# Two work tiles for GpSimd, a one-pass range check and a new order of the steps in an RWKV kernel

## The chip, the cores and the metric

The kernel runs on one core of a Trainium2 chip. The metric is the device time of one execution in microseconds (us), taken as the median of several runs. The core has five engines, each of which works through its own list of instructions strictly in order: TensorE (PE in the profile, with its weight loads as PEld), VectorE (DVE), ScalarE (ACT), GpSimd (POOL) and SyncE (SP), which here only issues DMA transfers. An instruction whose input isn't ready holds up everything that stands behind it on its engine.

## The reference

A linear attention with a state (RWKV) over 768 time steps, and behind it a feed-forward layer that the program calls MoE. Cut to what is computed:

```python
for t in range(S):                       # 4 batches x 8 heads, state 40 x 40 each
    y[:, :, t] = einsum('bhd,bhde->bhe', r_t, state)
    Sa = einsum('bhde,bhe->bhd', state, a_t)
    state = state * w_t[:, :, None, :] - einsum('bhd,bhe->bhde', Sa, b_t)
    state = state + einsum('bhd,bhe->bhde', v_t, k_t)
x = y.transpose(0, 2, 1, 3).reshape(4, 768, 320)
x_prev = x shifted by one step in time
xk = mu_k * x + (1 - mu_k) * x_prev ;  xr = mu_r * x + (1 - mu_r) * x_prev
out = sigmoid(xr @ w_r) * (relu(xk @ w_k) ** 2 @ w_v)     # 320 -> 1024 -> 320
```

All is float32.

## The kernel before

**Chunks.** Time is cut into 12 chunks of 64 steps (`NK`, `C`). A chunk is worked on in two halves `p` of the batches, 16 batch-and-head pairs each. Inside a chunk the recurrence becomes matrix products and one triangular solve; only a chain of small products carries the state from one chunk to the next.

**What is prepared for a chunk k, per half.** `load_wab` brings w, a, b and k of the chunk in one transfer (`wab`, 836 KB, two buffers in all). `check` has ACT look whether w lies inside the range in which the chunk form is safe; it writes into the tile `pe` that the next instruction overwrites, and sums into `beyond`. `front` is four pieces on DVE: a running product of w (L295), its inverse and a scan backwards (L298, L299), the scaling of a (L305) and of b and k (L307). `psc` (scores, L322) has PE multiply them, and ACT and DVE copy the parts to `sn` and `az`. `pkt` (L337) transposes `kb`, which lies in the `wab` buffer and is its last reader. So the next `wab` load of that half waits for `pkt`.

**The triangular solve.** `tri_out` (L351) writes blocks of `sn` to DRAM (`tx`, 64 KB each, runs of 128 bytes), `tri` (L366) loads them back in another layout into `TA`, and GpSimd solves in `TD` with 60 small instructions (L367 to L380), `tri_store` (L356) writes `TD` out (`ty`), and `tri_back` (L360) brings it into `sn`. There is one `TA` and one `TD` for all chunks.

**The chain of a chunk** (`chain`, `put`): the links z (L402), T (L408), L (L414), U (L420) and s (L426), each for both halves, with a copy on ACT between one and the next. T and U read what `tri_back` wrote. `put` (L441) hands the values on, and GpSimd multiplies the carried state by the decay into `mc` (L449), which `pmt` transposes in the next chunk. `pgh` (L472) and `py` (L488, L493) form the chunk's output, and `send_x` (L510, L512) sends it into the tile `x`, five transfers in runs of 256 bytes.

**MoE.** `Mix` works on one chunk's `x`: three differences (`diff`, L140), six mixed tiles, and 18 units of PE work (eight `ph`, eight `pv` pairs, two `pr`, as the generator `products` cuts them). `advance` emits one unit and, where they lie ahead, one of the mixes. Its weights come as 18 pieces that `convert` turns from 64-bit numbers into two 32-bit halves (`some_weights`).

**The order** is written out by hand. `STEP` holds 25 slots, numbered from 0, that are run for every chunk k. A word is a call; its last digit is the half. `z T L U s` are the links, `put pmt pgh py` belong to chunk k. `psc` and `pkt` are for chunk k+2, `w` is `load_wab` and `Q` is `check` for k+3, `r` (`load_rv`, 416 KB) and `v` load for k+1. `to` is `tri_out` and `tl` the load and solve of `tri` for k+2, `ts` is `tri_store` and `tk` `tri_back` for k+1, `x` is `send_x`. `F` emits one piece of a front, `M` one unit of MoE (before chunk `LAG`, now and then a weight piece). Copies and masks are put off to the end of the slot (`later`).

**DMA.** All loads and stores of a step are issued by SP in the order of the slots. There are eight completion semaphores, used in turn, so a transfer is issued only when the one eight places ahead of it has landed.

## Time and profile before

| | us |
|---|---|
| median of 3 runs (809.21 to 810.81) | 810.1 |
| the profiled execution | 807.6 |
| its span, from the first to the last instruction | 805.9 |
| busy: PE / DVE / POOL / ACT | 553.7 / 445.7 / 416.0 / 330.4 |
| mean granted TensorE clock | 0.867 of full speed |

The profile gives for each engine its busy time, and for each wait what ended it. No engine is busy for more than 69% of the span, so the time is set by engines that wait for each other. A step of the main loop is the time from one chunk's link z to the next chunk's. The first link z starts 84.0 us into the span and the last at 727.3 us; the last matmuls end close to the end of the span. So there is a head of some 84 us, eleven steps, and a last step with its tail of 79 us.

### The profile page before, as it was taken

How to read it: one execution, taken by the hardware profiler on the slowest of the kernel's cores; microseconds unless marked ns; L12 is line 12 of the kernel's file. 1: busy time of each engine (PE TensorE's matmuls, PEld its weight loads, DVE VectorE, ACT ScalarE, POOL GpSimd, SP SyncE). 2: the span in 40 equal slices, each digit the busy share in tenths (PEclk: the TensorE clock that was granted, in tenths of full speed). 3: DMA queues.
4: the chain of work that ended last, by engine and by line, in shares of the span. 5: the costliest groups of instructions: out<-in, count | busy, mean ns of one | idle time of the engine just before them, and what ended most of it. 6: DMA issues, size and time to landing. Idle time of an engine off the chain costs nothing.

```text
span 805.9 us, 24880 instructions
## 1 busy us (share of the span) xinstructions
PE 553.7 (69%) x10658; PEld 502.4 (62%) x10658; DVE 445.7 (55%) x772; ACT 330.4 (41%) x841; POOL 416.0 (52%) x815
## 2 busy tenths in 40 slices
PE   0302276236459979598598598596698799898966
PEld 0201266235458869487587487585687688797865
DVE  3754687469457467285385275392384492443441
ACT  1222241243144564363453444552453553545433
POOL 4086286088185187295494483484583582840000
PEclk9999999996758989699699679799589779797979
DMA  5245823842822732823814714714715625232010
GB/s 122 51 112 109 185 64 57 200 107 63 155 60 51 146 70 53 176 60 47 188 28 77 158 31 88 145 39 75 149 40 95 130 49 91 63 72 62 2 39 21
DMA packets 120321, 71.16 MB, mean 88 GB/s; under 512 B 96547, under 2 KB 110843, under 8 KB 117707
## 3 DMA queue, kind: packets, MB, share of 16 engines
q1 hardware_dynamic: 117710, 63.00, 38.5%
q10 hardware_dynamic: 2493, 6.49, 3.1%
q8 instruction: 85, 1.39, 0.8%
q14 instruction: 33, 0.27, 0.1%
HBM read 52.98 MB, written 10.22 MB: 78 GB/s over the span
## 4 chain that ended last, share of the span: by engine, by line
PE 42%; DMA 21%; DVE 12%; POOL 8%; SPq 6%; ACT 6%; issue 5%; ACTq 0%; DVEq 0%
DMA wab<-in_wab_dram 12%; PE ph L113 12%; PE pv L113 8%; POOL ttmp L373 4%; POOL td L376 4%; DMA x<-xp 3%; PE py L488 3%; PE py L493 2%; PE pgh L472 2%; PE psc L322 2%; PE ch L408 2%; PE ch L414 2%; PE ch L426 2%; PE pr L113 1%; DMA ty<-td 1%
## 5 line engine op out<-in xcount | busy, mean ns | idle before, releaser
L373 POOL TENSOR_TENSOR ttmp<-ta,td 128x30 f32<-128x30 f32 (+4 forms) x360 | 189.7, 527 | 28.3
L376 POOL TENSOR_TENSOR td<-td,ttmp 128x30 f32<-128x30 f32 (+4 forms) x360 | 176.7, 491 | 28.2
L113 PE MATMUL ph<-xk,wkh 120*128 120x256 f32 x480 | 110.8, 332 | 96.0 <-ACT hf L91 66.5
L113 PEld LDWEIGHTS ph<-xk,wkh 120*128 120x128 f32 x480 | 82.8, 220 | 104.9 <-ACT hf L91 70.1
L367 POOL TENSOR_SCALAR_AFFINE_SELECT td<-ta 64x512 f32<-64x512 f32 x24 | 19.5, 813 | 243.3 <-DMA ta<-tx 227.4
L91 DVE TENSOR_TENSOR hl<-hf,hh 128x256 fp32r<-128x256 f32 x96 | 43.1, 449 | 150.9 <-ACT hh L91 144.2
L322 PE MATMUL psc<-az,wab 40*64 40x64 f32 x1536 | 39.0, 253 | 63.4 <-DVE wab L307 53.9
L91 ACT ACTIVATE hf<-ph 128x256 f32<-128x256 f32 x96 | 36.9, 384 | 98.3 <-PE ph L113 98.3
L322 PEld LDWEIGHTS psc<-az,wab 40*64 40x64 f32 x1536 | 33.7, 163 | 69.0 <-issue 55.0
L91 ACT ACTIVATE pe<-wab,limit 104x512 f32<-104x512 f32 x48 | 34.6, 721 | 100.6 <-DMA wab<-in_wab_dram 96.0
L113 PE MATMUL ph<-xk,wkl 120*128 120x256 f32 x288 | 73.6, 312 | 1.4 <-DMA xk<-xk 1.4
L113 PE MATMUL pv<-wvh,hh 128*128 128x320 f32 x192 | 70.8, 369 | 0.0
L113 PE MATMUL pv<-wvh,hl 128*128 128x320 f32 x192 | 63.9, 333 | 0.0
L113 PE MATMUL pv<-wvl,hh 128*128 128x320 f32 x192 | 63.7, 332 | 0.0
L113 PEld LDWEIGHTS ph<-xk,wkl 120*128 120x128 f32 x288 | 56.0, 222 | 1.9 <-DMA xk<-xk 1.9
L408 PE MATMUL ch<-zs,sn 32*32 32x40 f32 x768 | 23.4, 236 | 45.6 <-ACT zs L91 35.0
L408 PEld LDWEIGHTS ch<-zs,sn 32*32 32x32 f32 x768 | 21.5, 141 | 48.1 <-ACT zs L91 45.8
L295 DVE TENSOR_TENSOR_SCAN pe<-wab,first 104x520 f32<-104x520 f32 x24 | 32.8, 1366 | 22.9 <-ACT pe L91 22.9
L91 ACT COPY vu<-ch 32x320 f32<-32x320 f32 x96 | 40.0, 417 | 9.1 <-PE ch L408 6.8
L113 PEld LDWEIGHTS pv<-wvh,hh 128*128 128x128 f32 x192 | 40.0, 209 | 4.2
L402 PE MATMUL ch<-vu,az 128*64 128x40 f32 (+1 forms) x768 | 31.9, 257 | 14.8 <-DMA vu<-in_vt_dram 14.8
L91 ACT ACTIVATE hf<-hf 128x256 f32<-128x256 f32 x96 | 40.1, 417 | 3.0
(95 smaller groups left out, 1207.2 us busy)
## 6 DMA issues: line engine op xcount, KB each, us to landing
wab<-in_wab_dram SPq DMA_DIRECT2D x24, 835.7 KB
vr<-in_rvd_dram SPq DMA_DIRECT2D x24, 416.0 KB
ta<-tx SPq DMA_DIRECT2D x24, 256.0 KB
vu<-in_vt_dram SPq DMA_DIRECT2D x24, 256.0 KB
out_dram<-sig SPq DMA_DIRECT2D x48, 80.0 KB
tx<-sn SPq DMA_DIRECT2D x48, 64.0 KB
ty<-td SPq DMA_DIRECT2D x24, 128.0 KB
sn<-ty SPq DMA_DIRECT2D x48, 64.0 KB
```

The lines of the kernel that those rows point to most:

```text
L91: f(*args, **kw)
L113: nc.tensor.matmul(out, lhsT=left[i][g], rhs=right[j][g], start=start and k == 0, stop=stop and k == len(terms) - 1)
L295: nc.vector.tensor_tensor_scan(out=pe.rearrange("p x t -> p (x t)"), data0=w[:, 0:SP], data1=first, initial=0.0, op0=ALU.mult, op1=ALU.add)
L322: nc.tensor.matmul(to[64 * y:64 * y + 64, x], lhsT=kb[r0:r1, x, y], rhs=az[r0:r1, i, x], start=True, stop=True)
L367: nc.gpsimd.affine_select(out=TD[h], in_=TA[h, i::2], compare_op=ALU.is_gt, fill=0.0, base=-i, pattern=[[-2, 16], [1, 32]], channel_multip ...
L373: nc.gpsimd.tensor_tensor(out=tmp, in0=TA[:, s:s + 1, s + 1:].broadcast_to([128, rows, n]), in1=TD[:, 0:rows, s:s + 1].broadcast_to([128, ...
L376: nc.gpsimd.tensor_tensor(out=TD[:, 0:rows, s + 1:], in0=TD[:, 0:rows, s + 1:], in1=tmp, op=ALU.subtract)
L402: mm(c3[64 * i:64 * i + 64, x], lhsT=az[0:kr[i], i, x], rhs=vu[0:kr[i], i, x, 0:HD], start=(x == 0), stop=True, skip_group_check=(x > 0))
L408: mm(c3[a:a + 32, x], lhsT=sn[a:a + 32, x, 0:32], rhs=zs[a:a + 32, x], start=True, stop=True)
L414: mm(c3[a + 32:a + 64, x], lhsT=sn[a:a + 32, x, 32:64], rhs=vu[a:a + 32, i, x, 0:HD], start=False, stop=True, skip_group_check=True)
L426: mm(c3[r0:r1, x], lhsT=kt[:, i, x], rhs=vu[:, i, x, 0:HD], start=(x == 0), stop=True, skip_group_check=(x > 0))
L488: nc.tensor.matmul(y[r0:r0 + n, 2 * x + q], lhsT=mk[:, x, i, q, 0:n], rhs=r[:, x, i], start=(x == 0 and q == 0), stop=False, skip_group_ch ...
```

## The change

- `TA` and `TD` exist twice, and chunk k uses the pair k modulo 2.
- `check` is one pass: Square of w - 0.9, summed; the sums are compared with 0.8 at the end, and the padding in the input is 0.9. It was two passes of Relu against 0.6 and 1.6.
- `fronts` becomes one list in the order of the checks; `F` always takes the next piece of the oldest.
- `STEP` is rewritten: `psc` is at slots 7 and 9, right behind U, where it was at 10 and 13; `to` at 10 and `tl` at 14, ahead of both `w`, where they were at 16 and 20; `ts` and `tk` are behind `w0` and `r0`; the check of half 0 is at slot 23 and that of half 1 (`q`) at slot 1 of the next step, where their passes were at 19 and 20, and 23 and 24; F stands in slots 0 to 6 and 24. There are 19 M in it, where there were 20.
- MoE starts at slot 12 of chunk 1, where it started with chunk 2.
- The head is rewritten: the first loads are split, the fronts of one half are laid over the scores of the other, and the loads for chunks 0 to 2 come earlier.
- `kt` has four buffers, where it had six.

```diff
-LAG = 2
+MOE_FROM = (1, 12)

 STEP = [x.split() for x in (
-    "z0 z1 F", "M", "T0 T1 F", "M pmt0", "L0 L1 F", "M pmt1 F", "U0 U1", "M F", "s0 s1 put0 F", "M put1", "M psc0 v F",
-    "M pgh0 F", "M", "M psc1", "M py0 ts", "M pgh1", "M pkt0 to", "M py1", "M pkt1 tk w0", "M r0 Q0", "M tl w1 Q0", "M x r1",
-    "M", "M Q1", "M Q1")]
+    "z0 z1 F", "M F q1", "T0 T1 F", "M pmt0 F", "L0 L1 F", "M pmt1 F", "U0 U1 F", "M psc0", "s0 s1", "M psc1", "M put0 to",
+    "M put1 v", "M pgh0", "M", "py0 tl", "M pgh1", "M pkt0", "M py1 w0 r0", "M pkt1 ts", "M w1 r1", "M", "M tk", "M x",
+    "M Q0", "M F")]
...
-            TA = att.tile([128, 32, 32], F32, name="ta")
-            TD = att.tile([128, 16, 32], F32, name="td")
+            TAS = [att.tile([128, 32, 32], F32, name=f"ta{i}") for i in range(2)]
+            TDS = [att.tile([128, 16, 32], F32, name=f"td{i}") for i in range(2)]
...
-                later(0, nc.scalar.activation, out=d["pe"][:, :, 1:], in_=w, func=AF.Relu, scale=(-1.0, 1.0)[i],
-                      bias=limit[:, i:i + 1], accum_out=beyond[:, i, k, p:p + 1])
+                later(0, nc.scalar.activation, out=d["pe"][:, :, 1:], in_=w, func=AF.Square, bias=limit,
+                      accum_out=beyond[:, k, p:p + 1])
+                fronts.append((k, p, front(k, p)))
+
+            def front_some(n):
+                while n > 0 and fronts:
+                    if next(fronts[0][2], 1) is None:
+                        n -= 1
+                    else:
+                        fronts.pop(0)
...
-                    nc.sync.dma_start(ty[:, i::2], TD[64 * i:64 * i + 64])
+                    nc.sync.dma_start(ty[:, i::2], TDS[k % 2][64 * i:64 * i + 64])
...
-                tx = st.pop((k, "tx"))
+                tx, TA, TD = st.pop((k, "tx")), TAS[k % 2], TDS[k % 2]
...
-            AHEAD = dict(r=(1, load_rv), w=(3, load_wab), Q=(3, check_next), psc=(2, scores), pkt=(2, pkt))
+            AHEAD = dict(r=(1, load_rv), w=(3, load_wab), Q=(3, check), q=(2, check), psc=(2, scores), pkt=(2, pkt))
...
+            def to_scores(k):
+                for p in range(2):
+                    check(k, p)
+                    flush()
+                front_some(4)
+                psc(k, 0)
+                front_some(2)
+                flush()
+                pkt(k, 0)
+                front_some(2)
+                psc(k, 1)
                 flush()
...
-                    load_wab(0, p)
+                    load_wab(0, p, ((0, WP), (WP, WP + 3 * G * C)))
                 for j in range(2):
-                    load_w(j)
...
+                    load_w(j, nc.sync)
+                to_scores(0)
+                tri_out(0)
+                load_wab(1, 0)
+                pkt(0, 1)
                 flush()
                 some_weights(1)
                 tri(0)
...
+                load_wab(1, 1)
+                some_weights(2)
+                to_scores(1)
+                tri_out(1)
+                pkt(1, 1)
                 flush()
...
+                load_wab(2, 0)
                 load_v(0)
                 for p in range(2):
                     load_rv(0, p)
...
+                tri(1)
+                load_wab(2, 1)
...
+                some_weights(1)
                 tri_store(0)
-                tri(1)
                 tri_back(0)
...
                             if what == "M":
-                                if k >= LAG:
+                                if (k, n) >= MOE_FROM:
                                     advance()
-                                elif n % 2 == 0:
+                                elif n % 2 == 0 or k > 0:
                                     some_weights(1)
```

**Where it moves the transfers.** SP before, around the late slots of the step of chunk 4; `wab` is the load for chunk 7, `tx` and `ta` belong to the solve of chunk 6, `ty` and `sn<-ty` to that of chunk 5:

```order
L356 DMA ty<-td 1024x1x32 x2
L91 DMA xk<-xk 40x256
L351 DMA tx<-sn_4010 32x16x32 x4
L360 DMA sn_3158<-ty 32x16x32 x4
L277 DMA wab_0_4380<-in_wab_dram 104x2057
L91 DMA out_dram<-sig 64x320 x4
L389 DMA vr_0_4406<-in_rvd_dram 104x4x256
L366 DMA ta<-tx 64x1024 x2
L277 DMA wab_1_4493<-in_wab_dram 104x2057
L510 DMA x_4515<-xp_4211 40x12x64 x2
L512 DMA x_4515<-xp_4211 40x4x64 x3
L389 DMA vr_1_4522<-in_rvd_dram 104x4x256
```

The same place of SP in the changed program:

```order
L362 DMA tx<-sn_4029 32x16x32 x4
L394 DMA vu<-in_vt_dram 64x2x512
L395 DMA vu<-in_vt_dram 64x2x512
L90 DMA xr<-xr 40x256
L377 DMA ta_114<-tx 64x1024 x2
L277 DMA wab_0_4524<-in_wab_dram 104x2057
L400 DMA vr_0_4526<-in_rvd_dram 104x4x256
L367 DMA ty<-td_117 1024x1x32 x2
L277 DMA wab_1_4575<-in_wab_dram 104x2057
L400 DMA vr_1_4577<-in_rvd_dram 104x4x256
L371 DMA sn_3195<-ty 32x16x32 x4
L521 DMA x_4618<-xp_4336 40x12x64 x2
```

The store and load ahead of GpSimd's solve (`tx`, `ta`) now stand ahead of both `wab` loads and no longer behind the store `ty` of the solve before; `ty` has moved behind the first `wab` and `vr`, and its way back into `sn` behind the second ones.

**Where it moves VectorE's work.** DVE before, at the beginning of the step of chunk 5; `pe_0`, `wab_0` and `az_102` are front pieces of chunk 7, half 0, `diff` the first MoE work on chunk 4's `x`:

```order
L295 SCALAR_TENSOR_TENSOR pe_0_4408<-wab_0_4380,first 104x520
L140 TENSOR_TENSOR diff<-x_4515 120x256 x3
L298 RECIPROCAL inv<-pe_0_4408 104x8
L299 SCALAR_TENSOR_TENSOR wab_0_4380<-wab_0_4380,inv 104x519
L91 TENSOR_TENSOR hl<-hf,hh 128x256
L305 TENSOR_TENSOR az_102<-wab_0_4380,pe_0_4408 40x512 x2
L307 TENSOR_TENSOR wab_0_4380<-wab_0_4380 104x1024
L91 TENSOR_TENSOR hl<-hf,hh 128x256
L295 SCALAR_TENSOR_TENSOR pe_1_4551<-wab_1_4493,first 104x520
L298 RECIPROCAL inv<-pe_1_4551 104x8
L299 SCALAR_TENSOR_TENSOR wab_1_4493<-wab_1_4493,inv 104x519
L91 TENSOR_TENSOR zs_0_4564<-ch_118,mc_98 104x320
```

The same place in the changed program:

```order
L306 SCALAR_TENSOR_TENSOR pe_0_4634<-wab_0_4524,first 104x520
L309 RECIPROCAL inv<-pe_0_4634 104x8
L310 SCALAR_TENSOR_TENSOR wab_0_4524<-wab_0_4524,inv 104x519
L139 TENSOR_TENSOR diff<-x_4618 120x256 x3
L316 TENSOR_TENSOR az_101<-wab_0_4524,pe_0_4634 40x512 x2
L318 TENSOR_TENSOR wab_0_4524<-wab_0_4524 104x1024
L147 SCALAR_TENSOR_TENSOR xm<-diff,muk,x_4618 120x256
L306 SCALAR_TENSOR_TENSOR pe_1_4703<-wab_1_4575,first 104x520
L309 RECIPROCAL inv<-pe_1_4703 104x8
L310 SCALAR_TENSOR_TENSOR wab_1_4575<-wab_1_4575,inv 104x519
L90 TENSOR_TENSOR xk<-xm,xk 120x256
L147 SCALAR_TENSOR_TENSOR xm<-diff,muk,x_4618 120x256
```

`diff` has moved from behind the first piece of half 0's front to behind its second, and the whole front of half 1 now stands ahead of the state sums of the chain (`zs`), where its third piece stood behind them.

More of the change, by code (lines that the diff above doesn't have):

```diff
@@ L67, in rwkv_kernel @@
         nc.gpsimd.memset(inv, 0.0)
-        beyond = const.tile([EP, 2, NK, 2], F32, name="beyond")
-        limit = const.tile([EP, 2], F32, name="limit")
-        nc.gpsimd.memset(limit[:, 0:1], W_LO)
-        nc.gpsimd.memset(limit[:, 1:2], -W_HI)
+        beyond = const.tile([EP, NK, 2], F32, name="beyond")
+        limit = const.tile([EP, 1], F32, name="limit")
+        nc.gpsimd.memset(limit, -W_MID)
         BUFS = dict(ch0=1, ch1=1, sw=3, pv=2, ph=1)
@@ L213, in rwkv_kernel, with load_w @@
             bufs = {}
-            def load_w(j):
+            def load_w(j, queue=nc.scalar):
                 if j >= len(pieces):
@@ L219, in load_w @@
                 buf = bufs[j] = moe.tile([128, 4 * CW], I32, tag=("xr", "xk")[j % 2], name="wbuf")[:rows]
-                nc.scalar.dma_start(buf[:, 0:2 * w].rearrange("p (n two) -> p n two", two=2),
-                                    src[:, i:i + w].bitcast(I32).rearrange("p (n two) -> p n two", two=2))
+                queue.dma_start(buf[:, 0:2 * w].rearrange("p (n two) -> p n two", two=2),
+                                src[:, i:i + w].bitcast(I32).rearrange("p (n two) -> p n two", two=2))
             def convert():
@@ L551, in scores @@
             def scores(k, p):
-                for _ in fronts[p]:
-                    pass
+                while fronts and fronts[0][:2] <= (k, p):
+                    front_some(1)
                 psc(k, p)
-            def check_next(k, p):
-                n = st[k, p]["checked"] = st[k, p].get("checked", -1) + 1
-                check(k, p, n)
             DO = dict(put=put, pmt=pmt, pgh=pgh, py=py)
-            AHEAD = dict(r=(1, load_rv), w=(3, load_wab), Q=(3, check_next), psc=(2, scores), pkt=(2, pkt))
+            AHEAD = dict(r=(1, load_rv), w=(3, load_wab), Q=(3, check), q=(2, check), psc=(2, scores), pkt=(2, pkt))
             BOTH = dict(v=(1, load_v), to=(2, tri_out), tl=(2, tri), ts=(1, tri_store), tk=(1, tri_back), x=(0, send_x))
-            def checks(k, p):
-                for i in range(2):
-                    check(k, p, i)
+            def to_scores(k):
[9 more added lines that the diff above has]
+                psc(k, 1)
                 flush()
@@ L600, in rwkv_kernel @@
                     load_rv(0, p)
-                    checks(2, p)
+                tri(1)
+                load_wab(2, 1)
+                for p in range(2):
                     some_weights(2)
+                    check(2, p)
+                    flush()
+                    for _ in range(2):
+                        next(fronts[-1][2])
+                some_weights(1)
                 tri_store(0)
-                tri(1)
                 tri_back(0)
@@ L607, in rwkv_kernel @@
                     chains = [chain(k, p) for p in range(2)]
-                    fronts = [front(k + 2, p) for p in range(2)] if k + 2 < NK else []
-                    if k == LAG:
-                        some_weights(100)
                     for n, slot in enumerate(STEP):
+                        if (k, n) == MOE_FROM:
+                            some_weights(100)
                         for what in slot:
                             if what == "M":
-                                if k >= LAG:
+                                if (k, n) >= MOE_FROM:
                                     advance()
-                                elif n % 2 == 0:
+                                elif n % 2 == 0 or k > 0:
                                     some_weights(1)
                             elif what == "F":
-                                any(next(x, 1) is None for x in fronts)
+                                front_some(1)
                             elif what in BOTH:
```

47 lines of the change are left out of this document (15 added, 32 removed).

## The prediction

> **What bounds the kernel now.** I read the sums of waits first, then the timelines of GpSimd and SP, then the chain. In the sums each row has the waiting instruction, what it waited for, us in total, times and the longest:
>
> ```profile
> POOL td L367 <- DMA ta<-tx: 227.4, 14, 30.1
> ACT pe L91 <- DMA wab<-in_wab_dram: 96.0, 16, 13.8
> PE ph L113 <- ACT hf L91: 66.5, 13, 14.4
> ```
>
> GpSimd waits for the input of its solve, ACT for `wab` in the range check, and PE for the ACT work queued behind that check. Between them stands a loop, seen in the timelines (start us, duration us, engine) where the step of chunk 4 passes into that of chunk 5:
>
> ```profile
> 278.91 1.80 POOL L367 TENSOR_SCALAR_AFFINE_SELECT td<-ta 64x512 f32<-64x512 f32 x2 [23.56 <-DMA ta<-tx]
> ...
> 335.83 0.83 POOL L367 TENSOR_SCALAR_AFFINE_SELECT td<-ta 64x512 f32<-64x512 f32 x1 [17.19 <-DMA ta<-tx]
> ...
> 374.77 1.44 POOL L91 TENSOR_TENSOR mc<-zs,pe 104x320 f32<-104x320 f32 x2
> ...
> 374.54 1.29 SPq L356 DMA_DIRECT2D ty<-td  x2
> ...
> 381.23 0.40 SPq L277 DMA_DIRECT2D wab<-in_wab_dram  x1
> 381.73 2.46 SPq L91 DMA_DIRECT2D out_dram<-sig  x4
> 384.24 0.94 SPq L389 DMA_DIRECT2D vr<-in_rvd_dram  x1
> 385.23 1.27 SPq L366 DMA_DIRECT2D ta<-tx  x2
> 388.48 0.33 SPq L277 DMA_DIRECT2D wab<-in_wab_dram  x1
> ...
> 630.93 0.71 POOL L367 TENSOR_SCALAR_AFFINE_SELECT td<-ta 64x512 f32<-64x512 f32 x1 [17.64 <-DMA ta<-tx]
> ```
>
> A solve starts at 335.8 and ends, with `mc`, at 376.2 (40.4 us). At its end SP stores `ty`, then `tx`, then fetches `ty` back, and only then, 6.7 us later, issues the first `wab` and, behind it, the next `ta`. From 278.91 to 630.93 are six rounds: **58.7 us** each. The chain of waits gives the landings and the link T of the next chunk:
>
> ```profile
> 381.23 7.18 DMA wab<-in_wab_dram
> 388.48 9.91 DMA wab<-in_wab_dram
> 400.50 2.34 PE ch L408 x64
> ```
>
> T comes 19.3 us after the first `wab` was issued. The step of chunk 9, whose end loads no `wab`, shows what follows:
>
> ```profile
> 621.67 0.50 SPq L277 DMA_DIRECT2D wab<-in_wab_dram  x1
> ...
> 624.10 11.52 SPq L512 DMA_DIRECT2D x<-xp  x3
> ...
> 636.19 0.72 ACT L91 ACTIVATE pe<-wab,limit 104x512 f32<-104x512 f32 x1 [2.72 <-DMA wab<-in_wab_dram]
> ...
> 638.16 1.45 DVE L140 TENSOR_TENSOR diff<-x 120x256 f32<-120x256 f32 x3 [3.04 <-DMA x<-xp]
> 638.22 1.34 PE L408 MATMUL ch<-zs,sn 32*32 32x40 f32 x64 [0.38 <-ACT zs L91]
> ...
> 670.34 0.69 PE L337 MATMUL pkt<-ident,wab 40*128 40x40 f32 x16
> ...
> 682.72 2.06 PE L402 MATMUL ch<-vu,az 128*64 128x40 f32 x64
> ...
> 727.26 0.96 PE L402 MATMUL ch<-vu,az 128*64 128x40 f32 x26
> ```
>
> From T and `diff` (both at 638.2) to the end of `pkt0` (671.0) are 32.9 us, in which VectorE does all the fronts, masks and mixes of a step. `x` lands 2.0 us after the second `wab` (636.2). So a step is 6.7 (SP behind the solve) + 19.3 (transfers) + 32.9 = 58.9, which is the 58.7 of the loop. I carry this sum over.
>
> **The change, part by part.**
>
> *Second TA and TD, `tx` and `ta` ahead of `ty` and `wab`.* The next solve no longer waits for the last one's way through SP. GpSimd's own loop is then the 40.4 us above, plus nothing, if `ta` lands before the solve ahead ends. The first `wab` of a step now waits only for `pkt0`: **6.7 us less per step**. What is late next is the transfers.
>
> *`ty` behind the first `wab` and `vr`, its way back behind the second.* Between the landings at 388.4 and 398.4 the queue moved 320 KB of `out`, 416 of `vr`, 512 of `ta` and 836 of `wab`: 209 KB per us. Counted from the first `wab`'s issue, it lands at 7.2; then `vr` 2.0, `ty` 1.2 (256 KB), `wab` 4.0, `vr` 2.0 and `sn<-ty` 1.2 make 17.6, say 18, the short runs being no faster than the rest. T needs `sn`, so it comes at 18. PE alone would be there at 15: in the step of chunk 9 `pkt0` ends at 671.0, z starts at 682.7 and takes 2.1, and one unit of MoE follows. So this wait takes the place of the old one, for 3 us, with everything on PE queued behind T. `x` follows with 360 KB, 1.7 us, and lands at 20; SP issues its third part only when the second `wab` is there (eight semaphores). Bounds for `x`: 15, if the transfers overlap and PE's own 15 counts, and 23, if the two 256 KB in short runs take twice as long.
>
> A rule of the Trainium skill speaks for the low end: "DMA: Bandwidth & Descriptors", section "Anatomy of one DMA", fits a transfer as 2.0 us plus its bytes at 436 KB per us. By it, as an estimate, the six transfers' 3016 KB would be in at 8.9 us, T would wait for nothing and the step would be rival B. The trace differs: 836 KB took 7.2 us and 2084 KB took 10.0. The page's fit is for another way of issuing; I go by the rows.
>
> *`diff`, fronts and scores.* `diff` still waits for `x`, and on VectorE the rest of both fronts is queued behind it, then the masks and `gh`, for which `py0` and so `pkt0` wait. As in chunk 9 this runs from `x` to `pkt0`: 32.9, less the second piece of half 0's front, now ahead of `diff` (1.3 for the scan that stood behind it, from the same length as the 1.25 of the scan quoted below), less one M between T and `pkt0` (1.15 us, a `ph` at full clock, quoted below): 30.5. The earlier slots of `psc` gain nothing while VectorE is late; if `x` were early, they would let PE go through.
>
> *The checks.* That of half 0 comes at slot 23, by the count of units, `py1` and `pkt1` some 9 us after `pkt0`, when its `wab` has landed (7.2). That of half 1, at slot 1, comes at about 14 and waits 1 us for a landing at 14.4; PE is waiting for `sn` then. The 96.0 us of ACT's wait go, and PE's 66.5 behind them, but both lay inside the loop and aren't counted a second time. One pass less saves 24 x 0.72 us (the row at 636.19) on ACT, hidden beside PE and VectorE.
>
> So a step takes 20 + 30.5 = **50.5 us**.
>
> *MoE from chunk 1.* With 12 units done in chunk 1 and 19 places for 18 units per step, what is left over at a step's start is 6, 5, 4, 3, 2, 1, 0, 0 units in chunks 2 to 9 (before: 36, falling by 2). Where it is 0, the new mix begins ahead of T, right after `x`. The price stands in the start of the last step, where that was so already (the first row is the `ph` used above):
>
> ```profile
> 249.57 1.15 PE ph L113 x8
> ...
> 728.64 1.11 DVE diff L140 x3
> ...
> 733.33 1.86 PE ph L113 x7
> ```
>
> From `diff` to the first `ph` 4.7 us, and 1.9 for it: T at 20 + 6.6 instead of 18. Then T to `pkt0` without the wait for VectorE, some 28: 54.6, or 4 more in chunks 8 and 9, and 1.5 in chunk 7, where it begins ahead of L. The eight steps from `pkt0` of chunk 1 to that of chunk 9: 5 x 50.5 + 52 + 2 x 54.6 = **413.7**.
>
> *The head.* Rows of the chain and of GpSimd:
>
> ```profile
> 1.75 9.59 DMA wab<-in_wab_dram
> ...
> 14.51 1.25 DVE pe L295
> ...
> 19.91 1.99 PE psc L322 x64
> ...
> 29.54 2.04 PE psc L322 x64
> ...
> 39.65 1.13 POOL L367 TENSOR_SCALAR_AFFINE_SELECT td<-ta 64x512 f32<-64x512 f32 x1 [30.14 <-DMA ta<-tx]
> ...
> 74.76 0.31 POOL L380 MEMSET td<- 64x16 f32 x2
> ...
> 82.97 11.60 DMA ty<-td
> ...
> 99.82 2.33 PE ch L408 x62
> ...
> 206.66 1.07 PE pkt L337 x15
> ```
>
> The first 217 KB land at about 6 instead of 11.3, so the first scan is at 8.5. A front takes 5.4 (14.51 to 19.91); two of them and the masks, without the wait for the first scores, bring the second scores to 20.7. The 10.1 us to the solve become 12.6, since 836 KB of `wab` now stand ahead of `ta`: solve from 33 to 68.5 (35.4 us as before). Then `ty` no longer follows loads issued right ahead of it (82.97, 11.60 us); with half that backlog and the 5.2 us from `sn<-ty` to T, T of chunk 0 is at 84 instead of 99.8 (78 to 92). Chunk 0: 30.5 to `pkt0` and 19 to the next T; chunk 1: 30.5 and 6.6 for a mix that starts all at once. `pkt0` of chunk 1 is at **171** (155 to 182, since weight pieces fill VectorE there in ways that I can't price) instead of 207.7.
>
> *From `pkt0` of chunk 9 to the end* 134.9 us (671.0 to 805.9) stay: two units of MoE fewer in chunk 10, one start of a mix more. The flag's extra instruction and `kt` with four buffers cost nothing: `py0` frees a buffer two slots before `pkt0` needs it.
>
> Sum: 171 + 413.7 + 134.9 = 719.6 us of span, against 805.9. The profiled execution was 1.7 above its span (807.6) and the median 2.5 above that: **724 us**.
>
> **The rivals.**
>
> *B: the transfers do overlap, and PE is the bound.* T at 15, nothing waits for `x`; a step is 15 + 29 = 44, above GpSimd's 40.4. Eight steps with 9 for late mixes: 361; time 671. For it: chunk 10 took 44.6 (682.7 to 727.3 for z), though with less work. Against it: 10.0 us between two landings, with the queue full.
>
> *C: the steps stay as they are*, because the change doesn't do what it says: with two `wab` buffers the load still waits for `pkt`, so it isn't further ahead, and only the head is gained. 171 + 463.3 + 134.9: 773. For it: 52 of the 58.7 us are left untouched by the second tile. Against it: the 6.7 are plain in SP's rows.
>
> *D: slower, by the clock.* PE now idles 3 to 10 us at T in every step, and after such a wait it was granted half its clock for long though busy all the time:
>
> ```profile
> 234.00:240.00 6.00, 6.00 (x103) 5.55 (x100) 4.90 (x9) 4.56 (x13) 5.29 (x10) 0.50 0.03 10
> 240.00:246.00 6.00, 6.00 (x81) 5.64 (x82) 3.92 (x7) 4.21 (x11) 5.14 (x12) 0.50 0.01 3
> ```
>
> (First PE's busy time in the stretch, the granted clock third from the end.) The old steps hold such stretches too, so only longer ones cost. If all of T to `pkt0` ran at half clock, up to 28 us more per step: 171 + 8 x 79 + 135 = 938. It is slower than before from 62.5 us per step on ((805.9 - 171 - 134.9) / 8), 11 more than the mean here: 22 us per step at half clock.
>
> "TensorE: Matmul & The Clock Gate" of the Trainium skill, Part 1, says that a busy window of about 3.4 us brings the full clock back. By that rule D would cost under 2 us a step and be out; the two rows above, 12 us of full work at half clock, don't agree, so D keeps its chance.
>
> **How the numbers follow.** Forecast (steps of 48 to 53): 0.55, 700 to 748. B 0.21, C 0.18, D 0.06. The range of 8 in 10 takes in most of B and C: 668 to 775. What a measurement can tell from no change is about 0.2%. A, B and C lie well below 808: faster 0.94, same 0.01, slower 0.05.
>
> **What would show it.** Right: the solve (L378 in the changed file) no longer waits long for `ta`; T (L419) waits for `sn<-ty`; `diff` waits for `x` in each of the steps 2 to 9; T to T near 50; solves back to back or nearly; first T near 84. Wrong: T waiting for `wab` through ACT, GpSimd idle 17 us per step as now (C), steps of 44 with no wait for `sn` (B), a mean clock below 0.75 (D). Wrong in size: the head, if weight pieces hold VectorE longer, and the last steps, if late mixes cost more than 4 us.

## The result and the profile after

The changed kernel takes 802.6 us (802.2 to 805.5, five runs). The kernel before took 809.2 in the same session: ratio **0.992**, 95% interval 0.990 to 0.994. The prediction was 724, range 668 to 775: the side is right, the size is far off. Of every run further below one execution was profiled, for e9_m18 the fastest of its four (730.3 us), for e5_x_early the slowest (857.3 us). The profiled execution of the changed kernel, whose span is 800.8 us, beside the terms of the prediction (a step is named after the chunk whose `pkt0` starts at its end):

| us | before | predicted | after |
|---|---|---|---|
| T of chunk 0 | 99.8 | 84 | 98.2 |
| `pkt0` of chunk 1 | 206.1 | 171 | 204.3 |
| steps of chunks 2 to 6 | 58.0 on average | 50.5 each | 49.6, 50.7, 51.9, 55.6, 59.6 |
| step of chunk 7 | the same | 52 | 61.8 |
| steps of chunks 8, 9 | the same | 54.6 each | 62.3, 61.4 |
| `pkt0` of chunk 9 to the end | 135.6 | 134.9 | 143.5 |

The measured times go by the start of `pkt0`; the prediction's own 207.7 and 134.9 went by its end, some 0.7 us later or more. Of the old T of chunk 0, two of the 64 matmuls start at 98.1 already. The head is 33 us longer than predicted, the eight steps 39, the end 9: together the 81 us between 719.6 and 800.8. Against the kernel before, the 24 us won in chunks 2 to 5 (4 x 58.0 less 207.8) mostly go again in chunks 6 to 9 (13 us) and at the end (8).

The page after: busy us, share of the span and instructions of each engine.

```profile
PE 571.1 (71%) x10658; PEld 516.7 (65%) x10658; DVE 433.5 (54%) x773; ACT 313.4 (39%) x793; POOL 373.5 (47%) x814
```

PE is busy for 17 us more than before (553.7) for the same products, at a mean granted clock of 0.806 instead of 0.867. The sums of waits after (waiting instruction, what it waited for, us in total, times, longest):

```profile
POOL mc L90 <- DVE zs L90: 171.9, 13, 45.8
...
POOL td L378 <- DMA ta<-tx: 139.2, 20, 24.5
...
DVE diff L139 <- DMA x<-xp: 61.4, 10, 8.3
PE ph L112 <- ACT xk L90: 61.0, 17, 12.4
...
PE ch L419 <- ACT zs L90: 44.6, 2, 24.0
...
PE ch L419 <- DMA sn<-ty: 30.5, 11, 5.3
...
ACT pe L90 <- DMA wab<-in_wab_dram: 17.8, 8, 4.1
```

The same four waits before:

```profile
POOL mc L91 <- DVE zs L91: 31.4, 1, 31.4
...
PE ph L113 <- ACT xk L91: 27.8, 8, 14.9
DVE diff L140 <- DMA x<-xp: 27.7, 9, 7.3
...
PE ch L408 <- DMA sn<-ty: 10.7, 2, 9.2
```

The wait of ACT for `wab` is down from 96.0 to 17.8. GpSimd's wait for `ta` is down from 227.4 to 139.2, and its wait for `zs` is up from 31.4 to 171.9: its solve is done early and `mc` waits for the chain, so it no longer bounds the step. T waits for `sn` and `diff` for `x`, as foreseen. Not foreseen in this size is PE's wait for `xk`, 61.0 us where it was 27.8. PE's timeline shows it, in the steps of the chunks 4, 7 and 8 (start us, duration us, engine, line, in brackets the idle time before and what ended it):

```profile
315.70 2.06 PE L413 MATMUL ch<-vu,az 128*64 128x40 f32 x64
...
324.11 0.30 PE L419 MATMUL ch<-zs,sn 32*32 32x40 f32 x2 [4.97 <-DMA sn<-ty]
...
501.67 0.58 PE L112 MATMUL ph<-xk,wkh 120*128 120x256 f32 x1 [7.34 <-ACT xk L90]
...
545.93 2.06 PE L413 MATMUL ch<-vu,az 128*64 128x40 f32 x64
560.36 0.58 PE L112 MATMUL ph<-xk,wkh 120*128 120x256 f32 x1 [12.36 <-ACT xk L90]
...
563.46 2.34 PE L419 MATMUL ch<-zs,sn 32*32 32x40 f32 x64
...
566.32 0.63 PE L112 MATMUL ph<-xk,wkl 120*128 120x256 f32 x2
...
582.20 0.40 PE L112 MATMUL ph<-xk,wkl 120*128 120x256 f32 x2
```

In chunk 4 PE waits 5.0 us for `sn` and goes on with T. In chunk 7 T still comes in time, at 491.4, but the first `ph` of the next MoE stands between T and L and waits 7.3 us for its mix. In chunk 8 that first `ph` stands ahead of T and waits for a mix whose `x` has only just landed; T starts 17.5 us after z instead of 8.4. Behind the gap the same pair of matmuls takes 0.63 us at 566 and 0.40 at 582: for 21.6 us, until 582.0, PE works at half its clock. The stretches of that kernel by step, and its last two (stretch, length, busy time of PE, PEld, DVE, ACT, POOL, then the granted clock, the DMA share and GB/s):

```profile
204.00:254.00 50.00, 42.67 (x903) 38.52 (x902) 30.57 (x57) 25.70 (x65) 21.12 (x49) 0.90 0.53 106
305.00:357.00 52.00, 45.20 (x906) 40.83 (x902) 31.59 (x54) 24.80 (x64) 36.86 (x73) 0.87 0.52 105
412.00:472.00 60.00, 49.38 (x906) 44.21 (x906) 31.10 (x55) 24.75 (x64) 31.82 (x67) 0.80 0.46 89
534.00:596.00 62.00, 48.38 (x894) 43.83 (x892) 30.45 (x54) 24.39 (x64) 27.39 (x65) 0.75 0.43 86
657.00:725.00 68.00, 58.66 (x948) 53.13 (x946) 26.07 (x53) 27.12 (x71) 24.04 (x64) 0.83 0.37 67
725.00:801.00 76.00, 61.43 (x787) 56.51 (x786) 23.15 (x53) 30.96 (x80) 1.48 (x2) 0.79 0.07 18
```

The same 900 matmuls take 42.7 us of busy time in the first row and 48 to 49 in the third and fourth, and PE idles 7 us in the first, 11 to 14 in those.

### The profile page after: what moved, and what is told of

The parts are those of the page before. It is cut to its first block, busy times and chain, and to the rows that moved or that the text cites. A ratio compares the mean times of both kernels' runs of the same rounds, so it can differ in the third digit from the quotient of the medians.

```text
span 800.8 us, 24776 instructions
## 1 busy us (share of the span) xinstructions
PE 571.1 (71%) x10658; PEld 516.7 (65%) x10658; DVE 433.5 (54%) x773; ACT 313.4 (39%) x793; POOL 373.5 (47%) x814
## 4 chain that ended last, share of the span: by engine, by line
PE 34%; DMA 28%; DVE 12%; SPq 9%; POOL 8%; issue 4%; ACT 3%; DVEq 0%; POOLq 0%; ACTq 0%
DMA ty<-td 10%; PE ph L112 9%; DMA ta<-tx 7%; PE pv L112 5%; SPq L371 4%; PE psc L333 4%; POOL td L387 3%; DMA x<-xp 3%; POOL ttmp L384 3%; PE ch L437 3%; PE ch L431 2%; PE ch L425 2%; SPq L521 2%; PE ch L419 2%; DMA wbuf<-in_w_v_dram 2%
## 5 line engine op out<-in xcount | busy, mean ns | idle before, releaser
L387 POOL TENSOR_TENSOR td<-td,ttmp 128x30 f32<-128x30 f32 (+4 forms) x360 | 165.3, 459 | 28.2
L384 POOL TENSOR_TENSOR ttmp<-ta,td 128x30 f32<-128x30 f32 (+4 forms) x360 | 161.2, 448 | 28.3
L112 PE MATMUL ph<-xk,wkh 120*128 120x256 f32 x480 | 115.5, 340 | 62.9 <-ACT xk L90 61.0
L90 POOL TENSOR_TENSOR mc<-zs,pe 104x320 f32<-104x320 f32 x24 | 18.6, 790 | 172.1 <-DVE zs L90 171.9
L419 PE MATMUL ch<-zs,sn 32*32 32x40 f32 x768 | 29.9, 263 | 75.2 <-ACT zs L90 44.6
L378 POOL TENSOR_SCALAR_AFFINE_SELECT td<-ta 64x512 f32<-64x512 f32 x24 | 17.6, 732 | 139.5 <-DMA ta<-tx 139.2
L419 PEld LDWEIGHTS ch<-zs,sn 32*32 32x32 f32 x768 | 27.2, 164 | 78.6 <-ACT zs L90 44.9
L90 DVE TENSOR_TENSOR az<-psc,mask 64x512 f32<-64x512 f32 x48 | 33.1, 689 | 41.5 <-PE psc L333 40.9
L90 ACT COPY vu<-ch 32x320 f32<-32x320 f32 x96 | 40.0, 416 | 27.5 <-PE ch L419 25.9
L139 DVE TENSOR_TENSOR diff<-x 120x256 f32<-120x256 f32 x36 | 16.6, 511 | 61.5 <-DMA x<-xp 61.4
L90 DVE TENSOR_TENSOR gh<-pgh,mask 128x512 f32<-128x512 f32 x48 | 30.9, 685 | 27.1 <-PE pgh L483 27.1
```

Source lines behind the costliest of these rows:

```text
L90: f(*args, **kw)
L112: nc.tensor.matmul(out, lhsT=left[i][g], rhs=right[j][g], start=start and k == 0, stop=stop and k == len(terms) - 1)
L139: nc.vector.tensor_tensor(out=d4[:, g], in0=x[:, g, :, 1:], in1=x[:, g, :, 0:C], op=ALU.subtract)
L378: nc.gpsimd.affine_select(out=TD[h], in_=TA[h, i::2], compare_op=ALU.is_gt, fill=0.0, base=-i, pattern=[[-2, 16], [1, 32]], channel_multip ...
L384: nc.gpsimd.tensor_tensor(out=tmp, in0=TA[:, s:s + 1, s + 1:].broadcast_to([128, rows, n]), in1=TD[:, 0:rows, s:s + 1].broadcast_to([128, ...
L387: nc.gpsimd.tensor_tensor(out=TD[:, 0:rows, s + 1:], in0=TD[:, 0:rows, s + 1:], in1=tmp, op=ALU.subtract)
```

## The experiments

All edit the changed kernel. Ratios are to the kernel before, run on the same chip in the same session; `head` is the start of `pkt0` of chunk 1, `steps` from there to `pkt0` of chunk 9, `end` the rest of the profiled span. These three are of the profiled execution.

| run | us | ratio (95%) | head | steps | end |
|---|---|---|---|---|---|
| the change | 802.6 | 0.992 (0.990 to 0.994) | 204.3 | 453.0 | 143.5 |
| e1_moe2 | 771.4 | 0.949 (0.935 to 0.964) | 193.2 | 446.2 | 127.8 |
| e2_moe2_m20 | 776.4 | 0.956 (0.941 to 0.970) | 192.8 | 447.0 | 137.2 |
| e9_m18 | 738.1 | 0.911 (0.903 to 0.918) | 202.5 | 413.8 | 112.3 |
| e13_fresh | 847.9 | 1.045 (1.043 to 1.047) | 208.9 | 494.1 | 137.2 |
| e14_m18_late | 750.2 | 0.923 (0.922 to 0.925) | 191.3 | 430.1 | 126.8 |
| e3_ts_early | 791.8 | 0.975 (0.961 to 0.988) | 203.5 | 445.3 | 140.9 |
| e5_x_early | 853.5 | 1.045 (1.037 to 1.052) | 206.3 | 501.5 | 147.8 |
| e6_x_ts | 795.3 | 0.978 (0.974 to 0.983) | 203.4 | 447.0 | 140.9 |
| e10_m18_ts | 726.6 | 0.895 (0.889 to 0.901) | 204.0 | 408.4 | 112.7 |
| e16_x_wab | 683.3 | 0.841 (0.837 to 0.844) | 195.1 | 374.0 | 112.1 |
| e17_x_wab_q | 671.6 | **0.826 (0.821 to 0.831)** | 200.4 | 358.7 | 112.2 |
| e4_head | 809.2 | 0.996 (0.992 to 1.001) | 206.0 | 457.1 | 144.5 |
| e7_x_ts_moe_head | 755.6 | 0.931 (0.926 to 0.936) | 189.7 | 440.4 | 119.6 |
| e11_m18_ts_head | 724.0 | 0.890 (0.884 to 0.896) | 203.1 | 408.3 | 113.0 |
| e12_m18_ts_head_w | 724.0 | 0.889 (0.883 to 0.895) | 203.2 | 409.8 | 112.3 |
| e8_one_tile | 818.7 | 1.008 (1.005 to 1.010) | 229.4 | 441.8 | 142.0 |
| e15_m18_ts_one | 726.3 | 0.893 (0.892 to 0.895) | 203.2 | 411.4 | 112.2 |

**Why the late steps are long.** First MoE was started later, then in the second run given a 20th place per step as well (the second diff comes on top of the first):

```diff
-MOE_FROM = (1, 12)
+MOE_FROM = (2, 0)
...
-    "M put1 v", "M pgh0", "M", "py0 tl", "M pgh1", "M pkt0", "M py1 w0 r0", "M pkt1 ts", "M w1 r1", "M", "M tk", "M x",
+    "M put1 v", "M pgh0", "M", "M py0 tl", "M pgh1", "M pkt0", "M py1 w0 r0", "M pkt1 ts", "M w1 r1", "M", "M tk", "M x",
```

> Only MOE_FROM is put back to (2, 0); the 19 places for MoE stay. Theory (a mix that starts close behind its x stalls PE inside the chain of links): with 36 units in hand at chunk 2 no step begins a mix on a fresh x. The steps from pkt0 of chunk 4 to that of chunk 9, 55.6, 59.6, 61.9, 62.3 and 61.4 us in the changed kernel, come to 50 to 52 each; 26 instead of 18 units are left for the tail, 9 us more there. About 755 us in all. Rival (the late steps are long because of the transfers, whatever MoE does): they stay at 56 to 62, and the time rises to about 808 by the longer tail.

> MoE from chunk 2 as in e1, and a twentieth place for it, in slot 14. Theory: the tail is back at 18 units, 9 us less than in e1; a unit more per step costs nothing while PE and VectorE wait for sn and x, so about 748 us. If PE were what a step of 50 us waits for, each of the ten steps would be 1.15 us longer and the time that of e1.

The first gained 31 us, short of the theory and far from its rival: the late steps fell from 60 to 62 us to between 55 and 58, but three of the first four rose to between 54 and 60. So, by the profiled executions, only 7 us of the gain are in the eight steps; the head is 11 us shorter, and the end, meant to be 9 us longer, 16 shorter. With later switches transfers of MoE stand in SP's queue ahead of `sn` and `x`, in the step of chunk 6 the four stores of a chunk's output. A 20th unit changed little: the steps stay, and the end, meant to be 9 us shorter than in the first run, is 9 longer. What the place of the switch does by itself was left open, and three runs with 18 units a step settle it. A chunk has 18 units; with 18 places the switch stays where it starts:

```diff
-    "M put1 v", "M pgh0", "M", "py0 tl", "M pgh1", "M pkt0", "M py1 w0 r0", "M pkt1 ts", "M w1 r1", "M", "M tk", "M x",
+    "M put1 v", "M pgh0", "M", "py0 tl", "M pgh1", "M pkt0", "M py1 w0 r0", "M pkt1 ts", "M w1 r1", "", "M tk", "M x",
```

> The changed kernel with 18 MoE units a step instead of 19 (the M of slot 20 left out), which is what a chunk's MoE has: 8 ph, 6 second products, 2 gates and 2 last. Theory (with 19 units a step the switch to the next chunk's x, begun 12 units in, comes one unit earlier in every step: after 6 units in step 2, after none in step 8; there PE stands on the mix of an x that has just landed, 'PE ph L112 <- ACT xk' with up to 12.4 us, ahead of the chain, and the clock falls behind it): with 18 units the switch stays 7 units into each step, so all steps stay at the 49.6 to 51.9 us of chunks 2 to 4, the eight sum to 400 to 415 instead of 453; 7 more units are left for the end, some 15 us; the whole 765 to 780. Rival (the late steps are long because PE is throttled, or because of the landings, wherever the switch stands): steps of chunks 6 to 9 58 us and more, the whole 800 or more.

One letter less is worth 64 us by the medians, more than the theory asked for: the steps are 49.4 to 53.6, their sum 39 us less, and the end is 31 us shorter where it was expected to be longer. Rows of the stretches (as above), two steps and the last two stretches:

```profile
256.00:305.00 49.00, 42.70 (x880) 38.88 (x878) 30.76 (x53) 24.44 (x63) 33.41 (x67) 0.86 0.54 108
464.00:516.00 52.00, 45.89 (x884) 41.84 (x880) 30.48 (x53) 24.54 (x63) 33.42 (x66) 0.80 0.51 102
616.00:664.00 48.00, 48.00 (x983) 44.49 (x983) 22.55 (x45) 27.31 (x72) 26.98 (x66) 1.00 0.50 95
664.00:729.00 65.00, 55.31 (x812) 51.83 (x804) 27.82 (x66) 33.96 (x88) 1.43 (x2) 0.96 0.11 27
```

In chunk 10, with 7 units left over, PE runs without a pause, 48.0 of 48 us at full clock; in the changed kernel the switch on a fresh `x` also stood in chunks 10 and 11, where PE waited 3.3 us each for `xk`, with 20 us of half clock behind each.

The next two keep the 18 units and their order of the slots, and move the switch: to the very start of each step, on a fresh `x` (two units at each M of step 1), or 14 units into it, on an `x` that landed some 30 us before. What moves with it are the places of MoE's own transfers in SP's queue. The first lines are e13_fresh's, the last pair e14_m18_late's.

```diff
                                 if (k, n) >= MOE_FROM:
+                                    if k == 1 and advance():
+                                        end_slot()
                                     advance()
...
-MOE_FROM = (1, 12)
+MOE_FROM = (1, 20)
```

> 18 MoE units a step, but two at each M of step 1, so that chunk 0's MoE is used up there and every later step begins with the x that has just landed (switch after 0 units, as step 8 of the changed kernel has it). Units per step, landings and all else as in the run with 18 units. Theory (it is the switch on a fresh x ahead of the chain that made the late steps long): PE waits 8 to 12 us for xk in every step, T at t+26 to t+31, steps of 58 to 62 us from chunk 2 on, sum of the eight 465 to 495, the whole 785 to 815. Rival (it was the 19th unit's own work on PE, the place of the switch costs little): steps of 50 to 54 us as with 18 units, the whole 725 to 750.

> 18 MoE units a step, begun only at slot 20 of step 1, so that the switch stays 14 units into each step, onto an x that landed some 40 us before; the last stores of each chunk's MoE then stand between wab and x in SyncE's queue, as in the run with MoE from step two (steps of 54 to 58 us there). Theory (only a switch on a fresh x is dear): steps of 50 to 53 us, no wait of PE for xk, the whole 735 to 755 (7 more units at the end, 12 us, against the run with 18 units). Rival (the stores in front of sn or x delay them and the step): T at t+21 to t+25, steps of 55 to 58 us, the whole 765 to 790.

With the switch on a fresh `x` every step from chunk 2 to 9 takes 56 to 64 us, T comes 29 to 31 us behind `pkt0`, and the kernel is slower than before the change. PE's timeline of that run:

```profile
404.16 2.06 PE L413 MATMUL ch<-vu,az 128*64 128x40 f32 x64
420.67 0.58 PE L112 MATMUL ph<-xk,wkh 120*128 120x256 f32 x1 [14.45 <-ACT xk L90]
...
423.75 2.34 PE L419 MATMUL ch<-zs,sn 32*32 32x40 f32 x64
```

With it 14 units in the steps take 53.8 on average. So **the place of the switch costs 8 us a step** (61.8 less 53.8; 10 against e9_m18's 51.7), with no unit more or less in it. In e13_fresh the stores stand behind `x`, and T waits for the `ph` ahead of it, not for `sn`. The whole, 847.9, is above the theory's 815. In e14_m18_late the rival has a part: 2 us a step against e9_m18, with T at t+20 to t+22 from chunk 3 on (t is the start of `pkt0`); in SP's queue the stores stand ahead of `sn`.

**What sets the 50 us.** The solved blocks were stored and fetched earlier, `x` was sent earlier, or both (one `+` line for each of the three runs):

```diff
-    "M put1 v", "M pgh0", "M", "py0 tl", "M pgh1", "M pkt0", "M py1 w0 r0", "M pkt1 ts", "M w1 r1", "M", "M tk", "M x",
+    "M put1 v", "M pgh0 ts", "M", "py0 tl", "M pgh1 tk", "M pkt0", "M py1 w0 r0", "M pkt1", "M w1 r1", "M", "M", "M x",
...
+    "M put1 v", "M pgh0", "M", "py0 tl", "M pgh1", "M pkt0", "M py1", "M pkt1 x w0 r0 ts", "M w1 r1", "M", "M tk", "M",
...
+    "M put1 v", "M pgh0 ts", "M", "py0 tl", "M pgh1 tk", "M pkt0", "M py1", "M pkt1 x w0 r0", "M w1 r1", "M", "M", "M",
```

> Only ts goes to slot 12 and tk to slot 15, ahead of both wab loads; the solve is over by then (it ends some 20 us before pkt0). Theory (T waits for sn<-ty behind the wab loads): T comes at 15 to 16 us after pkt0 instead of 19.6, x lands 2 to 3 us earlier than its 21.4, and a step of the chunks 2 to 4 takes 47 instead of 50 to 52; about 775 us. Rival (VectorE's wait for x alone sets the step): T comes earlier, but the steps shrink by no more than 2 us; about 787.

> The changed kernel with x sent right after py (slot 18), ahead of the two wab, the two vr, ty and sn in SyncE's queue; all else as in the change. Theory (the landing of x sets the step: diff at t+21 holds VectorE, t being the start of pkt0, and with it the masks and evacuations that PE waits for; the late steps are long because the mix on the fresh x comes after that wait): diff runs at t+8 to t+11, T stays at t+19 to t+21 since ty and sn stand no earlier, the way from T to pkt0 stays at 30 to 31 us in all steps instead of growing to 42, the eight steps of chunks 2 to 9 take 50 to 52 us each instead of 49.6 to 62.3: sum 400 to 416 instead of 453, the whole about 760 us (750 to 770). Rival (the late steps are long because PE has more MoE work in them and the granted clock falls; x only hides in it): late steps stay at 58 to 62 us, sum 440 or more, the whole 790 or more.

> As the run before it (x sent right after py), and the solved blocks stored at slot 12 and fetched back at slot 15, so that sn stands ahead of x, wab and vr in SyncE's queue. Theory (the two landings, sn and x, are all that holds the step after the change): T at t+14 to t+15 as in the run that only stored early (14.2 to 15.5), diff at t+8 to t+12, T to pkt0 30 to 32 us, steps of 45 to 47 us, sum of the eight 360 to 376, the whole 710 to 730 us. Rival (PE, ScalarE and VectorE with the MoE work set about 50 us per step, whatever lands when): T to pkt0 grows to 35 or more, steps stay at 50 to 55, sum 400 to 440, the whole 755 to 790.

Early `sn`: T at t+14 to t+15.5 in the chunks 2 to 7, and the way from T to `pkt0` longer by nearly as much; in the chunks 8 and 9, where the switch stands ahead of T, T still comes at t+27.5. Early `x`: some 50 us slower, against its theory. With `x` ahead of them, both `wab`, `ty` and with it `sn` come later, and T waits for `sn`; the sums of waits of that run, as above:

```profile
PE ch L419 <- DMA sn<-ty: 100.9, 12, 27.9
ACT pe L90 <- DMA wab<-in_wab_dram: 69.2, 13, 7.5
```

Nor did `diff` run before t+19, though `x` was sent at t+4.5 to t+8: it stands on VectorE behind the first pieces of a front, whose `wab` now lands late. Both early: no better than `sn` alone. The switch was still in its place there, so the earlier `sn` was tried again with 18 units:

```diff
+    "M put1 v", "M pgh0 ts", "M", "py0 tl", "M pgh1 tk", "M pkt0", "M py1 w0 r0", "M pkt1", "M w1 r1", "", "M", "M x",
```

> As the run before it, with the solved blocks stored at slot 12 and fetched back at slot 15. Theory (once the switch is in its place, the wait of the third link for sn is what is left: T from t+19.6 to t+14.5, and the step follows): steps of 45 to 48 us, the whole 735 to 755. Rival (PE itself, with 43 to 45 us of work at a granted clock of 0.87 and some 7 us of idle time that no landing ends, sets about 50 us): steps of 49 to 52 us, the way from T to pkt0 longer by what T gains, the whole within 8 us of the run before it.

T comes at t+13.3 in every step from chunk 2 on but one, and still the step is 51: the rival holds for the step. (The medians differ by 11.6 us, the two profiled spans, 728.6 and 725.1, by 3.5: e9_m18's executions spread from 730 to 743.) Its timeline shows two gaps in the place of one:

```profile
475.87 1.83 PE L425 MATMUL ch<-vu,sn 32*32 32x40 f32 x64 [3.32 <-ACT vu L90]
...
485.32 1.94 PE L431 MATMUL ch<-zs,sn 32*32 32x40 f32 x51 [5.03 <-ACT zs L90]
...
474.27 0.72 ACT L90 ACTIVATE pe<-wab,limit 104x512 f32<-104x512 f32 x1 [5.04 <-DMA wab<-in_wab_dram]
...
478.73 1.53 DVE L139 TENSOR_TENSOR diff<-x 120x256 f32<-120x256 f32 x3 [8.09 <-DMA x<-xp]
```

L waits for a copy on ACT that stands behind the check of half 1's `wab`, and U for one behind the mix, that is behind `diff` and `x`. The last two runs move these two landings (and have the head of e11_m18_ts_head): `x` between the two `wab`, `vr` behind them; then also the check of half 1 at slot 3.

```diff
+    "M put1 v", "M pgh0 ts", "M", "py0 tl", "M pgh1 tk", "M pkt0", "M py1 w0", "M pkt1 x", "M w1", "", "M r0", "M r1",
...
-    "z0 z1 F", "M F q1", "T0 T1 F", "M pmt0 F", "L0 L1 F", "M pmt1 F", "U0 U1 F", "M psc0", "s0 s1", "M psc1", "M put0 to",
+    "z0 z1 F", "M F", "T0 T1 F", "M pmt0 q1", "L0 L1 F", "M pmt1 F", "U0 U1 F", "M psc0", "s0 s1 F", "M psc1", "M put0 to",
```

> 18 MoE units a step, solved blocks stored at slot 12 and fetched at slot 15, the new head, and in SyncE's queue behind pkt0: wab of half 0, x, wab of half 1, then the two vr (before: wab, vr, wab, vr, x). In the run without the new place of x (step 51.5 us) T no longer waits, but L waits 3.3 us for ScalarE, which waits 5.0 for wab of half 1, and U waits 5.0 for ScalarE behind VectorE's diff, which waits 8.1 for x; the granted clock is half from 477 to 495 us. Theory (those two landings are what is left, and with them goes the half clock): no wait for x, half 1's wab lands 2 us sooner, the gaps at L and U fall below 3 us, steps of 44 to 48 us, the whole 680 to 705 us. Rival (one gap of PE of some 4 us per step is enough for the half clock, and the fronts on VectorE leave one): steps of 49 to 52 us, the whole 712 to 728.

> As the run before it, with the range check of half 1 at slot 3 instead of slot 1 and its front's pieces at slots 4, 5, 6 and 8. Theory (the wait of ScalarE for that wab, ahead of the copies that L needs, is a part of the gap): 1 to 3 us less per step than the run before it, the whole 8 to 24 us less. Rival (the later front delays psc and, through it, the rest): within 4 us of it, or slower.

The steps are 43.9 to 49.3 (46.8 on average) and then 43.6 to 46.8 (44.8), and the times are those of both theories; `diff` comes at t+14 to t+17. Two things that the first theory forecast did not come: PE's gap at L stayed at 3.2 to 4.7 us from chunk 3 on, and each step still has 7 to 17 us at half clock, as its rival had it. In the second run the gap has moved to U for most steps, 2.2 to 3.2 us, with 7 to 14 us at half clock. The second is the fastest version of the study, faster than both kernels. Two of its steps:

```profile
295.00:340.00 45.00, 42.13 (x900) 38.61 (x899) 31.66 (x53) 25.44 (x67) 34.72 (x66) 0.92 0.57 113
385.00:430.00 45.00, 42.23 (x889) 38.67 (x886) 32.34 (x53) 24.57 (x63) 34.49 (x66) 0.89 0.56 116
```

PE is busy for 42 of 45 us, at a granted clock of 0.92 and 0.89: this is the bound that is left.

**The head.** First `ty` and `sn` of the first solve were put ahead of `vr` and the last `wab`; then they stood ahead of the last `wab` only (`vr` kept its place, unlike what the expectations of those runs say), and the check of that `wab` was left to slot 1 (in e7_x_ts_moe_head with e6_x_ts's order and MoE from step two, in e11_m18_ts_head with e10_m18_ts's); then two weight pieces were left to step 1. Shown are the edits of the first and the last:

```diff
+                tri(1)
+                some_weights(2)
+                tri_store(0)
+                tri_back(0)
                 for p in range(2):
                     load_rv(0, p)
-                tri(1)
                 load_wab(2, 1)
...
-                                elif n % 2 == 0 or k > 0:
+                                elif n % 2 == 0 and n < 21 or k > 0:
```

> Only in the head: the store of the first solve and its way back are issued ahead of the two vr loads and the last wab load, behind which they wait now (issued at 72.6, back at 90.9). Theory (this backlog sets the first T): T of chunk 0 at 84 to 87 instead of 98.2, and the gain reaches the end: about 790 us. Rival (T of chunk 1, which waits for z's copy behind weight pieces on ScalarE, sets the rest): T of chunk 0 earlier, T of chunk 1 still near 161, and no more than 3 us gained.

> As the run before it, with MoE from step two (slot 0) as in the kernel before, and in the head the first solve's ty and sn ahead of the vr loads and the last wab, and the range check of that wab no longer in the head but in slot 1 of step 0. Theory on the head (in the run that only moved ty and sn nothing was gained because ScalarE, in order, waited until 97.3 us for that wab before it copied zs of the first link, whose matmuls ended at 77.5): T of chunk 0 at 80 to 90 us instead of 98, pkt0 of chunk 1 10 to 18 us earlier than in the run that started MoE at step two (193), and late steps of 45 to 50 us: the whole 690 to 715 us. Rival on the head (the weight pieces on ScalarE's queue set the first two steps whatever T does): pkt0 of chunk 1 within 5 us of 193.

> As the run before it, with the new head (first solve's ty and sn ahead of vr and the last wab, whose range check moves from the head to slot 1 of step 0). Theory (T of chunk 0 moves from 98 to 92 as in the run with MoE from step two, and some of it reaches pkt0 of chunk 1): pkt0 of chunk 1 at 198 to 202 instead of 204, the whole 3 to 7 us less than the run before it. Rival (the weight pieces on ScalarE's queue take the head's gain back): within 2 us of it.

> As the run before it, with the last two weight pieces of step 0 (slots 22 and 24) left to step 1. Theory (the third link of chunk 1 waits 24.0 us on ScalarE's copy of zs, which stands behind those pieces, whose loads land some 9 us each): T of chunk 1 at 140 to 150 instead of 157 to 161, pkt0 of chunk 1 8 to 15 us earlier, the whole less by as much. Rival (the pieces are bound by their loads and only stand somewhere else, now in step 1's chain): pkt0 of chunk 1 within 4 us of the run before it, or later.

The first move gained nothing. Its timeline shows why: z is done at 77.5, but its copy stands on ACT behind the check of a `wab` that lands at 97.

```profile
97.33 0.72 ACT L90 ACTIVATE pe<-wab,limit 104x512 f32<-104x512 f32 x1 [6.88 <-DMA wab<-in_wab_dram]
...
98.05 0.73 ACT L90 COPY zs<-ch 128x320 f32<-128x320 f32 x2
98.50 0.74 PE L419 MATMUL ch<-zs,sn 32*32 32x40 f32 x16 [21.03 <-ACT zs L90]
```

In the changed kernel the same copy stood behind that check (at 90.6, without a wait) and a weight piece:

```profile
97.26 0.51 ACT L239 CAST wkh<-wbuf 120x384 fp32r<-120x384 f32 x1 [3.72 <-DVE wbuf L237]
...
98.15 2.34 PE L419 MATMUL ch<-zs,sn 32*32 32x40 f32 x64 [20.68 <-ACT zs L90]
```

Without that check in the head T comes at 92 to 94, of which 1 to 4 us reach `pkt0` of chunk 1 (e7_x_ts_moe_head against e1_moe2, e11_m18_ts_head against e10_m18_ts). With two pieces moved, T of chunk 1 comes at 139.6 instead of 155.3, and `pkt0` of chunk 1 at the same 203.2: the pieces only stand between the next links. By `pkt0` of chunk 1 the rivals on the weight pieces hold. What would shorten the conversion itself wasn't tried.

**The second pair of work tiles.** One pair, for `TA` in the same way:

```diff
-            TDS = [att.tile([128, 16, 32], F32, name=f"td{i}") for i in range(2)]
+            TDS = [att.tile([128, 16, 32], F32, name=f"td{i}") for i in range(1)]
```

> The run that stored the solved blocks early (791.8 us), with one pair of GpSimd work tiles instead of two. Theory (after the change GpSimd is not the bound: its solve ends some 20 us before pkt0, so the second pair buys nothing in this order): 788 to 797 us, steps within 1 us of those with two pairs. Rival (with one pair the load of ta waits for the store and the solve slips onto the path, as in the kernel before, whose loop was 58.7 us): steps of 58 us and more in chunks 2 to 5, the whole 815 or more.

> 18 MoE units a step, solved blocks stored at slot 12 and fetched at slot 15, and one pair of GpSimd work tiles; in the head the first solve is stored before the second begins. Theory (the step of 51.5 us leaves one pair time enough: the solve takes 37 us, the store and the load of ta some 12): steps within 1 us of the run with two pairs (sum 408), T of chunk 0 at 95 to 100, the whole within 6 us of its 726.6. Rival (the loop of GpSimd with one pair, 58.7 us in the kernel before, binds again): steps of 53 us and more, the whole 745 or more.

The first run went as neither theory said in the head and as the first said in the steps on average (their sum is 441.8 against 445.3 with two pairs; single steps differ by up to 4 us). With one pair, its head stores the first solve only after the second has run in the same tile, so chunk 0 waits, and works with chunk 1's solved blocks; this is a fault of the edit, and its 27 us say nothing on the tiles. The second run stores first and is level with two pairs, 726.3 against 726.6.

## Why the prediction was wrong in size

- **New waits: right.** T waits for `sn` and `diff` for `x`, solves no longer bound the step, and chunks 2 to 4 take 49.6 to 51.9 us for 50.5. That the sum fits this well is partly luck: `diff` came 1.4 to 2.4 us later than forecast, and the way from there to the next `pkt0` was up to 3.4 us shorter.
- **Late mixes: the step that failed.** "T at 20 + 6.6 instead of 18 ... 54.6, or 4 more in chunks 8 and 9, and 1.5 in chunk 7" was priced from one start in the old kernel. The count of units left (6, 5, 4, 3, 2, 1, 0, 0) and the mechanism, a mix on a fresh `x` ahead of a link, were right; its price was not. The steps were 10.9 to 11.8 us over 50.5 in chunks 7 to 9, and it began in chunk 5 (5.1) and 6 (9.1), for which the prediction had put nothing. T came in time in the chunks 5 to 7, but PE waited 3.1, 4.7 and 7.3 us for `xk` between T and L, and from T to `pkt0` it took 35.8, 39.9 and 42.2 us for 32.4 in chunk 4. In chunk 8 T came at t+30 and not 26.6, and from T to `pkt0` it took 32.4 us and not 28, with PE at half clock for 18.5 of them. e13_fresh, e9_m18 and e14_m18_late show the place of the switch as the cause.
- **"stay": wrong for the end.** The term from `pkt0` of chunk 9 on was taken over at 134.9 with "one start of a mix more". Those starts cost more: 143.5, and 112.3 where 18 units leave a stock.
- **The head: mis-sized.** T of chunk 0 was to come at 84 by a smaller backlog; the order on ACT, with the check and a weight piece ahead of the copy that T needs, held it at 98.2. From there 106 us to `pkt0` of chunk 1, predicted as 87, went into weight pieces on VectorE and ACT; the prediction said that it couldn't price these.
- **GpSimd: right in effect, not by the tiles.** That 6.7 us go from the loop was put to the second pair together with the order. With 18 units and the solve stored early, one pair does the same. For the change's own order, in which the next solve overwrites the tile before `ts`, one pair can't be tried. No run takes the one-pass check, the earlier `psc` or the order of the fronts out alone; what each is worth stays open.
- **Rival B** (44 us a step, PE the bound) was right about the bound and wrong about what stands before it: e17_x_wab_q gets there, 44.8 a step, once the landings and the switch are out of PE's way. **Rival D** did not decide, but its mechanism is in every step looked at: the half clock behind a gap. **Rival C** fell: its 773, and its 463 for the eight steps against 453.0, came closer to the result than the forecast by size alone; the steps weren't as they were, but 49.6 to 62.3 us long and held by other waits.

The 18-unit version's steps sum to 413.8, the predicted 413.7, but by luck: 51.7 each, where five of 50.5 and three longer ones were meant.

## What to carry to other kernels

Where work of a side pipeline fills gaps in a main chain, count its units per step against the places for them: one place too many lets the side work catch up with its source, and then it waits in order ahead of the chain. Price such a wait by everything that stands behind it on the engine and by the clock that the gap costs. Moving one of several landings only shows the next one; look for all the gaps of the bounding engine in one step before moving any.
